# Two edits in a fused attention and gated-MLP training step: an early O^T load, and one finished input-gradient row per product

## The chip, the cores and the metric

The kernel runs on one core of one Trainium2 chip. A core has TensorE (PE, matrix products into PSUM), VectorE (DVE), ScalarE (ACT), GpSimd (POOL) and SyncE (SP). Here SP only starts DMA transfers, among them those that transpose while they copy; POOL starts the plain ones and does a few tiny copies. The metric is the device time of one execution in microseconds (us).

## The reference, cut to what matters

```python
xn = layernorm(x)                          # x: 2048 x 576
q = (xn @ wq) in 32 heads of 128           # k_cache, v_cache: 32 x 2048 x 128
p = softmax(q k^T / sqrt(128));  o = p v   # per head
s = concat(o) @ wo                         # 2048 x 4096 times 4096 x 576
g = silu((sigmoid(xn @ w_gate) * (xn @ w_up)) @ w_down)
out_0 = x + s * g
out_1..out_8 = vjp for x, k_cache, v_cache, wq, wo, w_gate, w_up, w_down of grad_out
```

So the kernel does the forward pass and the whole backward pass. out_1 is the gradient of the input x, and it goes back through the layernorm. out_4 is the gradient of wq, out_5 that of wo.

## The kernel before, in words

The 2048 rows are 16 row tiles of 128 (NT = 16). The stages, in order of time:

1. Up to about 3535 us: layernorm, the gated MLP's forward pass, and then attention, forward and backward, head by head. For each head it writes O and dQ in natural layout to DRAM (`on2_d`, `dq2_d`).
2. The O*wo stage, about 3535 to 3687 us. For each row tile, s = O wo is a sum over 32 heads (L957), each a pair of matmuls 512 and 64 columns wide. The stationary operand is O^T, so each row tile's O (128 x 4096, 1 MB) is loaded with a transposing DMA (`load_oT`, issued on SP, shown at L584).
3. The MLP's backward pass, in 18 column blocks, about 3687 to 4552 us.
4. The gradients of wq and wo and the rest of the input gradient, in 8 groups of 4 heads (NHG = 8, HG = 4), to the end.

**The O*wo stage.** Three O^T tiles rotate in memory whose contents are dead by now: row tile 0's lies in KQ, row tile 1's in xnT, row tile 2's in xn_all (the profile shows these names). KQ's first load is issued during attention. The wo rows of 23 heads (`h_early`) were loaded during attention, into dsT and xnT; those of the other nine (`h_late`) go to Kn, Vn and dOn, which attention still reads, so they are loaded in this stage (L575, on POOL). PE's order is written by hand: the early heads of row tile 0, the early heads of row tile 1, then the late heads of row tile 0, `close(0)`, the early heads of row tile 2, the late heads of row tile 1, and so on; from row tile 3 on a tile's heads go in one run. `close(st)` evicts the sums, starts the load of O^T for row tile st+3 into the same buffer, and forms out_0.

Before the first loads POOL issues `row_loads(0)` (three small row loads: dsg, g2b, xb). Then, for row tiles 1 and 2, it does a one-element copy from a loaded row into the O^T tile (L941), and only then is that O^T tile loaded: the copy makes SP's transposing load wait until the small load has landed. POOL issues the late wo rows after both copies.

**The last stage.** For each group of heads, SP loads the transposed wq columns (`wqT`, which lies in wdT's memory) and turns the dQ columns into `dqbT` four row tiles at a time (`turn_rows`; four calls for 16 row tiles). In every group PE does eight products of 32 matmuls (`accumulate`, L997): for each head one for wq's gradient (the result dqT is copied out by ACT, transposed into dwq by SP, and stored once a group by POOL) and one for wo's gradient (dwo, copied out by ACT and stored by POOL). Then it adds the group's part of the input gradient: 16 rows of `dx_more`, 8 matmuls each (L1053), which DVE adds to dxn.

In the last two groups rows are ended among the products. In group 6 (`early`) rows 0 to 7 get the parts of group 6 and of group 7 in one sum (16 matmuls), for which wqT2 and dqbT2, group 7's operands, are loaded ahead; rows 8 to 15 are added to dxn after the products. In group 7 (`final`) rows 8 to 15 get the last part and are ended. `finish` ends a row: on DVE tot and junk (two sums over the row), m12 and nb, then t; on ACT t again (scale and bias); on DVE dx; then POOL stores dx and loads a later row of grad_out. `ends_rows` decides when. It is called after each product but the last, and from product `wait_n` on it spreads the rows left over the places left, rounded up:

```python
if todo_rows and step_n >= wait_n:
    for _ in range(-(-len(todo_rows) // max(1, nsteps - step_n - final))):
```

With nsteps = 8, before: in group 6 (wait_n 5) after products 5, 6, 7: 3, 3, 2 rows; in group 7 (wait_n 2) after products 2 to 6: 2, 2, 2, 1, 1 rows.

The sums of products and rows rotate through four PSUM buffers. In these stages the program order fixes the instruction order on SP, POOL, DVE and PE; ACT's order is chosen by the scheduler when the program is built.

Of the kernel before, what the change touches and what calls it, by code (L numbers as in the profile page):

```python
# [66 lines left out]
def kernel(  # L67
# [6 lines left out]
    nc = tc.nc  # L74
# [6 lines left out]
    NT = S // P  # L81
# [152 lines left out]
    with tc.tile_pool(name="pa", bufs=1) as pa:  # L234
# [271 lines left out]
        with tc.tile_pool(name="a2h", bufs=3) as hp, \  # L506
# [4 lines left out]
            for sg in range(NT // SG):  # L511
# [7 lines left out]
                for sl in range(SG):  # L519
                    st = sg * SG + sl  # L520
# [358 lines left out]
    HG = ldiv(H, 4)  # L879
    NHG = H // HG  # L880
    WD = ncs[-1][0] + 512
    with late("pc") as pc, late("pcf") as pcf, \
# [22 lines left out]
        with late("c1l3", 4) as ldp3, late("c1s", 2) as sb, \  # L905
                late("c1ps", 3, space=PSUM) as ps, late("c1pt", 2, space=PSUM) as pst:
            if KPAD:
                nc.vector.memset(doBT[:LO, DT - 1, :], 0.0)

            def turn_do(st, pt):  # L910
                cols = slice(st * P, (st + 1) * P)
                for i in range(DT):
                    c0 = min(i * P, D - P)
                    nc.tensor.transpose(pt[:, i, :], doB[:, st, c0:c0 + P], ident[:])
                nf = DT - 1 if KPAD else DT
                if nf:
                    alt.copy(doBT[:, :nf, cols], pt[:, :nf, :], eng="s")
                if KPAD:
                    alt.copy(doBT[LO:, nf, cols], pt[LO:, nf, :], eng="v")

            wo_of = {}
            for view, h0, n, _ in wo_parts:
                for k in range(n):
                    wo_of[h0 + k] = view[:, k, :]
            h_early = [h0 + k for _, h0, n, dead in wo_parts if dead not in (1, 2, 3) for k in range(n)]
            h_late = [h0 + k for _, h0, n, dead in wo_parts if dead in (1, 2, 3) for k in range(n)]
            oTs.append(oT_view(xn_all[:].rearrange("p t d -> p (t d)"), 0))

            def row_loads(st):
                res = []  # L930
                for nm, src in (("dsg", dsg_d), ("g2b", g2_d), ("xb", x2)):
                    t_ = ldp3.tile([P, D], bf, name=nm)
                    nc.gpsimd.dma_start(t_[:], src[st * P:(st + 1) * P, :])
                    res.append(t_)
                return res

            R0 = min(3, NT)
            loads = {}
            loads[0] = row_loads(0)
            for st in range(1, R0):  # L940
                nc.gpsimd.tensor_copy(oTs[st][0:1, 0, 0:1], loads[0][st % 3][0:1, 0:1])  # L941
                load_oT(oTs[st], st)
            for view, h0, n, dead in wo_parts:
                if dead in (1, 2, 3):
                    load_wo_rows(view, h0, 0, n)
            for st in range(1, R0):
                loads[st] = row_loads(st)
            pend_tr = []
            accs_of = {}

            def mm(st, hs_):
                if st not in accs_of:
                    accs_of[st] = [ps.tile([P, 512], f32, name=f"acc{j}") for j in range(len(ncs))]
                oT = oTs[st % 3]
                for h in hs_:
                    for j, (n0, nn) in enumerate(ncs):
                        nc.tensor.matmul(accs_of[st][j][:, :nn], lhsT=oT[:, h, :], rhs=wo_of[h][:, n0:n0 + nn],  # L957
                                         start=(h == h_early[0]), stop=(h == (h_early + h_late)[-1]))

            def close(st):  # L960
                accs = accs_of.pop(st)
                dsg, g2b, xb = loads.pop(st)
                if st + R0 < NT:
                    load_oT(oTs[st % 3], st + R0)
                    loads[st + R0] = row_loads(st + R0)
                s_sb = sb.tile([P, D], f32, name="s_sb")
                for j, (n0, nn) in enumerate(ncs):
                    alt.copy(s_sb[:, n0:n0 + nn], accs[j][:, :nn], eng="s")
                nc.vector.tensor_tensor(doB[:, st, :], s_sb[:], dsg[:], op=ALU.mult)
                t0 = sb.tile([P, D], f32, name="t0")  # L970
                nc.vector.tensor_tensor(t0[:], s_sb[:], g2b[:], op=ALU.mult)
                nc.vector.tensor_tensor(xb[:], t0[:], xb[:], op=ALU.add)
                nc.gpsimd.dma_start(o0[st * P:(st + 1) * P, :], xb[:])
                pend_tr.append(st)

            for st in range(R0 - 1):
                mm(st, h_early)
            for st in range(NT):
                if st == NT - 3 or (st == 0 and NT < 3):
                    load_wdT(0)  # L980
                if st == NT - NT // 4:
                    load_blk(ah0[:, 0, :, :], a_d, 0)
                    load_blk(ah0[:, 1, :, :], h_d, 0)
                while len(pend_tr) > 1:
                    st_ = pend_tr.pop(0)
                    turn_do(st_, pst.tile([P, 8, P], bf, name="pt", tag="tr"))
                mm(st, h_late if st in accs_of else h_early + h_late)
                close(st)
                if st == 0 and R0 > 1:
                    mm(R0 - 1, h_early)  # L990
# [56 lines left out]
        def turn_rows(dst, src, a, b, n):  # L1047
            nc.sync.dma_start_transpose(dst[:, a * n:b * n, :], src[:, a:b, :].rearrange("p t f -> p (t f)"))
# [111 lines left out]
        with late("c2w") as wp, late("c2b") as blk, late("c2s", 2) as sb, late("c2ps", 4, space=PSUM) as ps:  # L1160
# [45 lines left out]
            for hg in range(NHG):  # L1206
                cols = slice(hg * HC, (hg + 1) * HC)
                onb, dqb = onqs[hg % 2]
                final = hg == NHG - 1
                early = hg == NHG - 2  # L1210
                ends = list(range(NTE)) if early else list(range(NTE, NT)) if final else []
                nc.sync.dma_start_transpose(wqT, A_wq[:, cols])
                for a in range(NTE if final else 0, NT, NQ):
                    turn_rows(dqbT, dqb, a, min(a + NQ, NT), HG)
                dwq = wp.tile([P, DT, HC], bf, name="dwq")
                for st in ends[:2]:
                    load_got(st)
                nsteps, step_n = 2 * HG, 0
                wait_n = min(5 if early else 2, nsteps - 2)
                todo_rows = list(ends)  # L1220
                held = []

                def ends_rows():
                    if todo_rows and step_n >= wait_n:
                        for _ in range(-(-len(todo_rows) // max(1, nsteps - step_n - final))):
                            if todo_rows:
                                st = todo_rows.pop(0)
                                finish(st, dx_more(st, early))
                                if st + 2 <= ends[-1]:
                                    load_got(st + 2)  # L1230
                for hl in range(HG):
                    h = hg * HG + hl
                    lcols = slice(hl * P, (hl + 1) * P)
                    accumulate(ps.tile([P, WD], f32, name="acc"), dqb, xn_all, lcols, dqTs[h % 2])
                    nc.sync.dma_start_transpose(dwq[:, :, lcols], dqTs[h % 2][:])
                    if early and hl == min(1, HG - 1):
                        nc.sync.dma_start_transpose(wqT2[:], A_wq[:, (hg + 1) * HC:(hg + 2) * HC])
                        turn_rows(dqbT2, onqs[(hg + 1) % 2][1], 0, NTE, HG)
                    if final and hl == HG - 1:
                        store_T(out_4, cols, dwq)  # L1240
                    step_n += 1
                    ends_rows()
                    dwo = sb.tile([P, D], bf, name="dwo")
                    accumulate(ps.tile([P, WD], f32, name="acc"), onb, ds_all, lcols, dwo)
                    nc.gpsimd.dma_start(out_5[h * P:(h + 1) * P, :], dwo[:])  # L1245
                    step_n += 1
                    if hl < HG - 1:
                        ends_rows()
                if not final:
                    if hg + 2 < NHG:  # L1250
                        load_on(onb, hg + 2)
                        load_dq(dqb, hg + 2)
                    store_T(out_4, cols, dwq)
                    for st in range(len(ends), NT):
                        acc = dx_more(st)
                        nc.vector.tensor_tensor(dxn[:, st, :], acc[:, :D], dxn[:, st, :], op=ALU.add)  # L1256
                while todo_rows:
                    step_n = nsteps
                    ends_rows()
# [30 lines left out]
```

## Time and profile before

| what | us |
|---|---|
| median of 4 runs | 4957.46 |
| the runs | 4955.02 to 4962.40 |
| the profiled execution's own time | 4957.68 |
| its span (first to last instruction) | 4955.9 |
| PE busy | 4839.2 |
| DVE busy | 2802.6 |
| ACT busy | 2472.1 |
| group 6 begins on PE | 4834.73 |
| group 7 begins on PE | 4903.69 |

How to read it: times in the trace count from the span's start. A line of a timeline has start, length, engine, line of the kernel, operation, output tile, input tiles, and, in brackets, how long the engine had been idle and what released it. A line of the waits has the engine and what it was about to do, the releaser, the total wait in us, the number of waits, and the longest. A line of the DMA issues has the tile, the queue, the count, the size where it is known, and the median us from issue to landing. The granted clock is the share of TensorE's full clock in a window. The rows' times come from one execution, so sums are made against its own time.

### The profile page before, as it was taken

The numbers are of one execution on the slowest core, as the hardware profiler recorded it, in microseconds if no ns is written. First come the engines' busy times: TensorE is split into PE (matmuls) and PEld (weight loads), VectorE is DVE, ScalarE is ACT, GpSimd is POOL, SyncE is SP. The second block draws the span as 40 slices with busy tenths as digits, with TensorE's granted clock in tenths as the row PEclk, the third lists the DMA queues.
The fourth block names the chain that finished last, engine by engine and source line by source line (L and its number), as shares of the span: only waits on it lengthen the run. The fifth ranks groups of instructions, "written<-read, shape, count | busy, mean of one in ns | idle before, by whom it ended". The sixth has DMA issues, their size and how long they took to land. (4 is left out here: it accounts for less than half of the span.)

```text
span 4955.9 us, 100870 instructions
## 1 busy us (share of the span) xinstructions
PE 4839.2 (98%) x40273; PEld 2895.1 (58%) x41029; DVE 2802.6 (57%) x6554; ACT 2472.1 (50%) x4228; POOL 840.8 (17%) x1330
## 2 busy tenths in 40 slices
PE   9999999999999999999999999999799999999998
PEld 4445666666666666666666666666455555555554
DVE  4544665666566566666666656656334555553224
ACT  4432766666766676676666666667212111111111
POOL 3322111111111111111111111111121111111111
PEclk9999999999999999999999999999899999999999
DMA  7887999999999999999999999999999999997765
GB/s 259 274 202 175 224 230 223 223 226 234 220 234 230 222 232 228 225 227 222 233 226 227 227 225 231 232 218 230 203 220 243 220 229 215 240 235 185 205 177 129
DMA packets 3048180, 1097.68 MB, mean 221 GB/s; under 512 B 2951889, under 2 KB 2956114, under 8 KB 3047698
## 3 DMA queue, kind: packets, MB, share of 16 engines
q1 hardware_dynamic: 2948930, 771.66, 83.3%
q0 software_dynamic: 98160, 318.85, 20.1%
q8 instruction: 322, 5.28, 0.4%
q14 instruction: 160, 1.31, 0.1%
q10 hardware_dynamic: 608, 0.59, 0.0%
HBM read 175.31 MB, written 177.93 MB: 71 GB/s over the span
## 5 line engine op out<-in xcount | busy, mean ns | idle before, releaser
L654 ACT ACTIVATE Pq<-sp 128x1024 bf16<-128x1024 f32 x1024 | 1047.0, 1023 | 269.4 <-PE sp L636 226.5
L709 DVE SCALAR_TENSOR_TENSOR Pq<-dp,negdelta,Pq 128x1024 bf16<-128x1024 f32 x512 | 655.2, 1280 | 42.4 <-PE dp L706 41.4
L712 ACT ACTIVATE t<-dp,negdelta 128x1024 bf16<-128x1024 f32 x512 | 567.1, 1114 | 214.5 <-PE dp L706 165.1
L683 PEld LDWEIGHTS <-dST 128*128 128x128 bf16 x8192 | 508.3, 98 | 150.9 <-DMA dST<-Pq 9.1
L706 PE MATMUL dp<-VT,dOT 128*128 128x512 bf16 x1919 | 581.6, 379 | 2.4
L683 PEld LDWEIGHTS <-PT 128*128 128x128 bf16 x8192 | 500.1, 98 | 135.5 <-DMA PT<-Pq 15.6
L636 PE MATMUL sp<-KQ 128*128 128x512 bf16 x1858 | 568.3, 379 | 2.2 <-ACT Pq L654 2.1
L683 PE MATMUL acc<-Kn,dST 128*128 128x128 bf16 x8192 | 557.1, 219 | 7.8 <-DMA dST<-Pq 5.9
L683 PE MATMUL acc<-Vn,PT 128*128 128x128 bf16 x8192 | 542.3, 219 | 12.6 <-DMA PT<-Pq 10.4
L744 PE MATMUL acc<-Pq,dOn 128*128 128x512 bf16 x1983 | 528.3, 379 | 10.2 <-issue 0.2
L713 DVE TENSOR_TENSOR Pq<-t,Pq 128x1024 bf16<-128x1024 bf16 x512 | 354.4, 692 | 318.9 <-ACT t L712 307.1
L744 PE MATMUL acc<-Pq,Qn 128*128 128x512 bf16 x2013 | 524.3, 380 | 4.9
L724 ACT ACTIVATE dq_n<-acc,rsc 128x128 bf16<-128x128 f32 x512 | 187.5, 366 | 332.5 <-PE acc L683 311.1
L1153 DVE TENSOR_TENSOR dxn<-acc,dxn 128x576 f32<-128x576 f32 x272 | 206.1, 758 | 248.1 <-PE acc L1053 248.1
L744 PEld LDWEIGHTS <-Qn 128*128 128x128 bf16 x2048 | 200.5, 98 | 240.9 <-issue 1.6
L744 PEld LDWEIGHTS <-dOn 128*128 128x128 bf16 x2048 | 199.2, 98 | 234.4 <-issue 1.1
L1115 ACT ACTIVATE ndh<-dh 128x512 bf16<-128x512 f32 x144 | 86.0, 597 | 452.5 <-DVE du_blk L1113 448.7
L706 PEld LDWEIGHTS <-dOT 128*128 128x128 bf16 x2048 | 178.9, 98 | 124.8 <-issue 12.7
L636 PEld LDWEIGHTS <-KQ 128*128 128x128 bf16 x2048 | 179.2, 98 | 124.1 <-issue 3.6
L641 DVE TENSOR_REDUCE rs_all<-rsp 128x1 f32<-128x2 f32 x512 | 78.4, 153 | 306.1 <-ACT Pq L654 294.6
L677 POOL DMA_DIRECT2D on_d<-o_n x128 | 97.1, 759 | 786.0 <-DVE junk L695 458.7
L677 POOL DMA_DIRECT2D dq_d<-dq_n x128 | 97.9, 765 | 718.1 <-ACT dq_n L724 678.3
(209 smaller groups left out, 6797.1 us busy)
## 6 DMA issues: line engine op xcount, KB each, us to landing
out_dram<-kvn POOLq DMA_DIRECT2D x64, 512.0 KB, 5.0
ah<-a_d POOLq DMA_DIRECT2D x18, 1024.0 KB, 9.2
ah<-h_d POOLq DMA_DIRECT2D x18, 1024.0 KB, 11.5
h_d<-h_row POOLq DMA_DIRECT2D x64, 256.0 KB, 3.5
a_d<-a_row POOLq DMA_DIRECT2D x64, 256.0 KB, 3.9
x_all<-in_A_k_cache_dram SPq DMA_DIRECT2D x64, 256.0 KB, 4.0
on_d<-o_n POOLq DMA_DIRECT2D x128, 128.0 KB, 4.6
kvT_d<-KQ POOLq DMA_DIRECT2D x32, 512.0 KB, 5.0
```

The costliest lines, as they stand in the source:

```text
L636: nc.tensor.matmul(sp[:, c * CH:(c + 1) * CH], lhsT=hs.QT[:, qt * P:(qt + 1) * P], rhs=hs.KT[:, hf * HW_ + c * CH: hf * HW_ + (c + 1) * CH ...
L654: nc.scalar.activation(Pq[:, hsl], sp[:], AF.Exp, scale=SCALE, accum_out=hs.rsp[:, hf:hf + 1])
L677: nc.gpsimd.dma_start(dst_d[q0 * P:(qt + 1) * P, hs.h * P:(hs.h + 1) * P].rearrange("(t p) d -> p t d", p=P), buf[:])
L683: nc.tensor.matmul(hs.acc[:, 0, :], lhsT=T[:, kt, :], rhs=rhs[:, kt, :], start=(kt == 0), stop=(kt == NT - 1))
L706: nc.tensor.matmul(dp[:, c * CH:(c + 1) * CH], lhsT=hs.dOT[:, qt * P:(qt + 1) * P], rhs=hs.VT[:, hf * HW_ + c * CH: hf * HW_ + (c + 1) * C ...
L709: nc.vector.scalar_tensor_tensor(Pq[:, hsl], dp[:], hs.negdelta[:, qt:qt + 1], Pq[:, hsl], op0=ALU.add, op1=ALU.mult)
L712: nc.scalar.activation(t[:], dp[:], AF.Identity, bias=hs.negdelta[:, qt:qt + 1], scale=1.0)
L713: nc.vector.tensor_tensor(Pq[:, hsl], t[:], Pq[:, hsl], op=ALU.mult)
L724: nc.scalar.activation(hs.dq_n[:, qt % G4, :], hs.acc[:, 0, :], AF.Copy, scale=hs.rsc[:, qt:qt + 1])
L744: nc.tensor.matmul(self.acc, lhsT=self.nat[:, qt, :], rhs=self.slabs[qt][:, cs], start=(qt == self.lo), stop=(qt == self.hi - 1))
L1115: nc.scalar.mul(ndh[:], dh[:], -1.0)
L1153: nc.vector.tensor_tensor(dxn[:, st, :], acc[:, :D], dxn[:, st, :], op=ALU.add)
```

## The change

In the O*wo stage, POOL's one-element copy is left out for row tile 1, so its O^T load no longer waits for a row load; row tile 2's is kept. In the last stage `wait_n` goes from 5 to 3 in group 6 and from 2 to 1 in group 7, so rows are ended after products 3 to 7 in group 6 (2, 2, 2, 1, 1 rows) and after products 1 to 6 in group 7 (2, 2, 1, 1, 1, 1). In group 6, SP's order is changed for that: the turns of dQ for rows 0 to 7, wqT2 and dqbT2 are issued at the group's start, and the turns for rows 8 to 15 after the second dwq transpose.

```diff
--- before.py
+++ after.py
@@ -938,7 +938,8 @@
             loads = {}
             loads[0] = row_loads(0)
             for st in range(1, R0):
-                nc.gpsimd.tensor_copy(oTs[st][0:1, 0, 0:1], loads[0][st % 3][0:1, 0:1])
+                if st > 1:
+                    nc.gpsimd.tensor_copy(oTs[st][0:1, 0, 0:1], loads[0][st % 3][0:1, 0:1])
                 load_oT(oTs[st], st)
             for view, h0, n, dead in wo_parts:
                 if dead in (1, 2, 3):
@@ -1210,13 +1211,18 @@
                 early = hg == NHG - 2
                 ends = list(range(NTE)) if early else list(range(NTE, NT)) if final else []
                 nc.sync.dma_start_transpose(wqT, A_wq[:, cols])
-                for a in range(NTE if final else 0, NT, NQ):
-                    turn_rows(dqbT, dqb, a, min(a + NQ, NT), HG)
+                def turn_dq(a, b):
+                    for a_ in range(a, b, NQ):
+                        turn_rows(dqbT, dqb, a_, min(a_ + NQ, b), HG)
+                turn_dq(NTE if final else 0, NTE if early else NT)
+                if early:
+                    nc.sync.dma_start_transpose(wqT2[:], A_wq[:, (hg + 1) * HC:(hg + 2) * HC])
+                    turn_rows(dqbT2, onqs[(hg + 1) % 2][1], 0, NTE, HG)
                 dwq = wp.tile([P, DT, HC], bf, name="dwq")
                 for st in ends[:2]:
                     load_got(st)
                 nsteps, step_n = 2 * HG, 0
-                wait_n = min(5 if early else 2, nsteps - 2)
+                wait_n = min(3 if early else 1, nsteps - 2)
                 todo_rows = list(ends)
                 held = []
 
@@ -1234,8 +1240,7 @@
                     accumulate(ps.tile([P, WD], f32, name="acc"), dqb, xn_all, lcols, dqTs[h % 2])
                     nc.sync.dma_start_transpose(dwq[:, :, lcols], dqTs[h % 2][:])
                     if early and hl == min(1, HG - 1):
-                        nc.sync.dma_start_transpose(wqT2[:], A_wq[:, (hg + 1) * HC:(hg + 2) * HC])
-                        turn_rows(dqbT2, onqs[(hg + 1) % 2][1], 0, NTE, HG)
+                        turn_dq(NTE, NT)
                     if final and hl == HG - 1:
                         store_T(out_4, cols, dwq)
                     step_n += 1
```

## The prediction

> **What bounds the kernel now.** I read the page first (what is busy), then PE's waits inside the two stages the diff touches, then the timelines of PE, SP and DVE there. The page:
>
> ```profile
> span 4955.9 us, 100870 instructions
> PE 4839.2 (98%) x40273; PEld 2895.1 (58%) x41029; DVE 2802.6 (57%) x6554; ACT 2472.1 (50%) x4228; POOL 840.8 (17%) x1330
> ```
>
> TensorE fills the span, so only what removes its idle time, or the tail after its last matmul, can pay. The waits of PE in the O*wo stage (3530 to 3690 us) and in the last two head groups (4834 to 4956):
>
> ```profile
> PE acc L957 <- DMA xnT<-on_d: 18.9, 1, 18.9
> ...
> PE acc L1053 <- DMA dqbT<-dqb: 3.8, 1, 3.8
> PE acc L1053 <- DVE dxn L1256: 3.2, 1, 3.2
> PE acc L1053 <- DVE tot L1192: 1.1, 1, 1.1
> ```
>
> The first line is the second O^T tile (its view lies in xnT's memory); the rest belong to group 6, the last but one. SP's own waits, and what was in flight from 3536 to 3562 (last number: us to landing):
>
> ```profile
> SPq L584 <- POOL xn_all L941: 10.9, 1, 10.9
> ...
> Kn<-in_A_wo_dram POOLq DMA_DIRECT2D x1, 432.0 KB, 9.6
> Vn<-in_A_wo_dram POOLq DMA_DIRECT2D x1, 432.0 KB, 12.8
> dOn<-in_A_wo_dram POOLq DMA_DIRECT2D x1, 432.0 KB, 13.3
> xnT<-on_d SPq DMA_TRANSPOSE x1, 17.9
> xn_all<-on_d SPq DMA_TRANSPOSE x1, 22.2
> ```
>
> SP issued xnT's load at 3542.40 and had been held 10.9 us by the Pool copy: it stood ready at 3531.5. PE's timeline of group 6 (start, length, last bracket the idle time before):
>
> ```profile
> 4854.33 1.14 PE L1053 MATMUL acc<-wdT,dqbT 128*128 128x512 bf16 x8
> 4859.24 2.10 PE L1053 MATMUL acc<-wqT,dqbT 128*128 128x512 bf16 x8 [3.77 <-DMA dqbT<-dqb]
> ...
> 4892.76 1.14 PE L1053 MATMUL acc<-wdT,dqbT 128*128 128x512 bf16 x7 [1.11 <-DVE tot L1192]
> 4897.10 6.75 PE L1053 MATMUL acc<-wdT,dqbT 128*128 128x512 bf16 x32 [3.20 <-DVE dxn L1256]
> 4903.69 4.08 PE L997 MATMUL acc<-xn_all,dqb 128*128 128x512 bf16 x31
> ```
>
> A product starts every 3.92 us, a half row (8 matmuls) every 0.98. After the 3.77 and the 3.20 wait matmuls run at half speed.
>
> **Part 1, O*wo.** Removed: one Pool copy (0.18 us, off the path) and SP's wait. The built order shows no other difference in this stage. SP is ready at 3531.5; the load's issue takes 4.89. Landing: 7.0 us at the least and 10.0 at the median for these loads, so 3538.5 to 3541.5. In flight beside it are only the kvT_d store (issued 3535.36) and the first row loads (3539.19). PE needs the tile when row 0's early part ends, 3541.5, so the 18.94 us wait goes (1 us left at most).
>
> What is late next: row 1's early 23 heads take 5.65 us, to 3547.2. Row 0's late heads then need the wo loads, which Pool still issues behind the copy for xn_all: Kn 3543.24+9.6=3552.8, Vn 3556.8, dOn 3558.0, then 0.74 us, 3558.8. Row 2's early part needs xn_all. Its load now goes out at 3543.0, where xnT's went before, into the same burst of wo and row loads. Upper bound: xnT's 17.9, landing 3560.9 (3562 if the row loads land 1 us later beside xnT). Lower: the median 10.0, but not before the late heads, 3555.5. Nearest row is the burst itself, with no second transpose queued behind it: I take 3559.7. Row 2's early part started at 3570.30 before: 10.6 earlier.
>
> A clock cost comes off. After its 18.94 us wait row 1's early part took 7.62 us (3560.47 to 3568.09) instead of 5.65: 2.0 lost, already in the old time. Now PE idles from 3547.2 to 3552.8 and works in pieces, so row 2's early part pays: 2.3 (2.0 to 3.4, half of the 6.8 us slow stretches seen). It ends at 3559.7+5.65+2.3=3567.65 against 3570.30+5.65=3575.95: **8.3 us gained**, between 4.9 (3562, 3.4) and 12.8 (3555.5, 2.0). Later rows lie beside their loads: row 3's load goes out when row 0 closes, near 3558.9, and landed 9.4 us after issue before, 3568.3, needed near 3572.5. Everything after shifts with PE, which had 1.9 us of waits in all from 3570 to group 6.
>
> The page "DMA: Bandwidth & Descriptors" of the Trainium skill (Queues, rings and completion order) says each DMA engine takes turns between queues packet by packet; here transposes move in packets under 512 B and wo loads in larger ones, so by that rule xn_all gains nothing from xnT's absence, lands at 3560.9, and this part's gain would be 7.1. The trace can't separate the two.
>
> **Part 2, group 6.** Matmuls and DVE's list are unchanged; two row pairs move ahead on PE, ACT's copies and Pool's dwo stores are reordered around the rows, and on SP wqT2 and dqbT2 pass two dqb turns and two dwq transposes. Pure PE work is 8x3.92+16x0.98+8x0.98=54.9; the group took 4903.69-4834.73=68.96: 14.1 lost (waits 3.77+1.11+3.20; half clock 7.74x0.38=2.9 after the first and 6.60x0.42=2.8 after the last, by the granted clocks below). New order on SP from 4834.93: wqT 3.77, two turns 2.03+1.96, wqT2 2.90, dqbT2 4.24, with gaps 4850.1; PE resumed 1.8 after dqbT2's issue ended, so 4851.9. PE has three products done at 4846.49 and a half row at 4847.47, so **it still waits, 4.4 instead of 3.8**, and pays the half clock once (2.9 as before, up to 3.4; I take 3.1). Rows then come two per product for three products, one for two, 34.9 us of DVE chain (8 rows of 4.36, below) beside 4851.9 to 4889: PE's four PSUM buffers, each freed by a row's tot or by ACT's copy, are free in time (the 1.11 and 3.20 waits were for them, behind three rows at once), so these waits and the second slow stretch go. If the chain lagged by one row again, 1.1 would be back. 54.9+4.4+3.1=62.4: **6.6 gained**. The dwq transposes that waited now end 4852.7, long before dqT's buffers are wanted (4869); the two delayed turns land at 4859, wanted at 4889. Pool's dwo stores stand behind two rows' stores instead of three, and dwo's two buffers are wanted two products later.
>
> ```profile
> 4925.12 0.76 DVE L1202 TENSOR_TENSOR dx<-t,got 128x576 bf16<-128x576 f32 x1 [0.99 <-ACT t L1200]
> 4925.80 0.75 DVE L1192 SCALAR_TENSOR_TENSOR tot<-acc,dxn 128x576 f32<-128x576 f32 x1
> ...
> 4929.47 0.76 DVE L1202 TENSOR_TENSOR dx<-t,got 128x576 bf16<-128x576 f32 x1 [0.99 <-ACT t L1200]
> ```
>
> One row holds DVE for 4.36 us, ACT's step included.
>
> **Group 7.** From its start: wqT 2.31, first turn 2.08, landing and restart 2.2 and gaps: the first rows' data are there at +6.85. PE is there at +3.92, one product earlier than before, so a **new wait of 2.9** appears; behind it PE holds seven products. The row chain starts at +8.05 instead of +9.02 (4912.71): 1.0 gained. The end gives it back: ACT's built order now puts the last dqT copy behind row 15's t. From that t's end: copy 0.62, dwq transpose 2.7 to landing, 0.3, two out_4 issues 1.3, then the dwo store, 4.9; before, 4946.87 to 4949.88, 3.0. So +1.9-1.0=**0.9 lost**, 1.5 if the new wait also slows PE, since the first row then takes up to 1 us longer.
>
> Weighing that: the windows show granted clock 0.62 after the 3.77 wait, 0.58 after the 3.20 wait, and 1.00 from 504.28 after a 2.33 wait; 2.9 lies between, even odds. "TensorE: Matmul & The Clock Gate" of the Trainium skill (Part 1) puts the drop at one idle window of about 3.4 us that runs freely, a rule that speaks against cutting a wait into new ones; by it 2.9 us would cost nothing and group 7 loses 0.9, by the nearest row (3.20) 1.5.
>
> Late stage: 6.6-1.2=5.4 gained, between 2.8 (dqbT2 2 us later, a slow stretch of 3.4, 1.5 in group 7) and 6.5 (dqbT2 0.8 sooner, 0.9 in group 7).
>
> **Sum.** The profiled execution took 4957.68 (span 4955.9), 0.2 over the median 4957.46. 4957.68-8.3-5.4=4944.0: **4944**.
>
> **Rivals.** (A) Forecast: 4938.4 to 4950 at the ends of both parts. (B) xn_all and the wo loads land later still, near 3565, and O*wo gives 3: 4949.3. For: both are still held, and 22.2 us to landing occurs. Against: in the trace that figure has xnT's load in front of it. (C) Group 6's wait grows by 5 (dqbT's longest landing is 10.0 us against a median of 4.3): 4949. For: dqbT2 now runs where two turns did. Against: the only large load near it, dqb's, landed at 4822.25+14.2=4836.5. (D) Slower: xnT in flight starves the first row loads, whose landing releases the Pool copy and so wo and xn_all. Its price is one for one; O*wo breaks even at a delay of 8.3 us, the whole change at 13.7. If xnT takes xn_all's 22.2 (to 3553.7) and the rows land after it, the copy is 13.7 late, O*wo loses 5.4, and with the late part at its 2.8 the time is 4960.3. Against: the DMA share is 0.40 from 3535 to 3541.5, not the burst's 1.01. (E) The load isn't early, since another wait holds SP: 4952.3. Against: its remaining waits are on stores and transposes of attention that landed by 3531.
>
> **Numbers.** A 0.78, B 0.08, C 0.08, D 0.03, E 0.03. A measurement of this kernel tells about 0.2% (9.9 us) from no change, so faster means under 4947.6. A lies there for 92 in 100, B and C for a third: 0.78x0.92+0.16/3=0.77. Slower by that much is the far end of D, 0.02; the rest, 0.21, is the same. The range, 4938 to 4951, runs from A's lower end over B and C; D, E and their neighbours are left out.
>
> **What would show it.** Right: xnT issued near 3531.5; PE's 18.9 wait replaced by one near 3547 for the wo loads, 5 to 12 us in all with xn_all; in group 6 one wait of 4 to 5 us on dqbT2, none on tot or dxn; in group 7 a wait near 3; out_4 issued last behind a late dqT copy. Wrong: xnT or the copy late, a PE wait on dqT or dwo copies, or more than two slow stretches in the late stage.

## The result, and the profile after

The changed kernel takes 4946.15 us (median of 44 runs, 4940.76 to 4958.83); the kernel before, run beside it, 4957.46 us (median of 65, 4946.28 to 4971.02). The ratio is 0.9978, 95% interval 0.9974 to 0.9982: faster by 0.22%, 11 us. The forecast was 4944 us, 13.7 less than the profiled execution of before. The profiled execution of the changed kernel took 4943.66 us.

The page, then PE's waits in the O*wo stage (3530 to 3690 us) and in the last two groups (4815 to 4942), after the change:

```profile
span 4941.8 us, 100865 instructions
PE 4836.5 (98%) x40273; PEld 2893.3 (59%) x41029; DVE 2802.9 (57%) x6554; ACT 2471.8 (50%) x4228; POOL 840.6 (17%) x1329
...
PE acc L958 <- issue: 4.7, 3, 3.2
PE acc L958 <- DMA Vn<-in_A_wo_dram: 3.4, 1, 3.4
PE acc L958 <- DMA Kn<-in_A_wo_dram: 2.4, 1, 2.4
PE acc L958 <- DMA xn_all<-on_d: 1.2, 1, 1.2
...
PE acc L1054 <- DMA dqbT<-dqb: 6.3, 2, 3.8
```

The 18.9 us wait for xnT is gone, and the waits for the wo loads and xn_all that the forecast put in its place are there: 5.8 and 1.2, 7.0 in all. Not forecast is "issue": three stops, the longest 3.2, in which PE waited for nothing that the profile shows. In the last two groups one wait of 3.8 (group 6) and one of 2.5 (group 7) are left, both for dqb turns.

Attention ends at another time in every execution (3526 to 3545 us here), so the stage is measured from there. The O*wo stretch, from attention's last matmul to the MLP backward's first, went from 153.30 to 147.93 us; group 6 from 68.96 to 61.45; group 7's start to the span's end from 52.19 to 53.23. So 5.4 + 7.5 - 1.0 = 11.9 us; attention, whose instructions the change does not touch, ended 2.2 us sooner in this pair. That the profiled time, 4943.66, falls on the forecast's 4944.0 is luck: without those 2.2 us it would lie 2 us above it.

### The profile page after: what moved, and what is told of

The parts are those of the page before. It is cut to its first block, busy times and chain, and to the rows that moved or that the text cites. A ratio compares the mean times of both kernels' runs of the same rounds, so it can differ in the third digit from the quotient of the medians.

```text
span 4941.8 us, 100865 instructions
## 1 busy us (share of the span) xinstructions
PE 4836.5 (98%) x40273; PEld 2893.3 (59%) x41029; DVE 2802.9 (57%) x6554; ACT 2471.8 (50%) x4228; POOL 840.6 (17%) x1329
## 4 chain that ended last, share of the span: by engine, by line
PE 93%; issue 2%; DMA 2%; DVE 2%; ACT 0%; SPq 0%; POOL 0%; POOLq 0%; ACTq 0%; DVEq 0%
PE acc L683 18%; PE acc L744 17%; PE acc L998 12%; PE acc L1054 8%; PE dp L706 8%; PE sp L636 8%; PE acc L215 6%; PE u_ps L450 3%; PE dh L1111 3%; PE g_ps L448 3%; PE acc L533 2%; PE acc L958 2%; PE acct L145 1%; DMA PT<-Pq 1%; DVE Pq L709 1%
## 5 line engine op out<-in xcount | busy, mean ns | idle before, releaser
L744 PE MATMUL acc<-Pq,dOn 128*128 128x512 bf16 x1983 | 527.8, 379 | 10.0
L744 PE MATMUL acc<-Pq,Qn 128*128 128x512 bf16 x2013 | 522.9, 379 | 4.9
L744 PEld LDWEIGHTS <-Qn 128*128 128x128 bf16 x2048 | 200.1, 98 | 240.0
L744 PEld LDWEIGHTS <-dOn 128*128 128x128 bf16 x2048 | 198.9, 98 | 234.2 <-issue 0.5
```

Source lines behind the costliest of these rows:

```text
L744: nc.tensor.matmul(self.acc, lhsT=self.nat[:, qt, :], rhs=self.slabs[qt][:, cs], start=(qt == self.lo), stop=(qt == self.hi - 1))
```

## The new stop behind attention

PE and POOL after the change (start, length; last bracket the idle time before), with the same places of the kernel before in the second fence; the L744 line ends attention:

```profile
3529.74 2.32 PE L744 MATMUL acc<-Pq,Qn 128*128 128x512 bf16 x10
...
3533.40 2.61 PE L958 MATMUL acc<-dsT,KQ 128*128 128x512 bf16 x20 [1.35 <-issue]
3539.23 2.56 PE L958 MATMUL acc<-dsT,KQ 128*128 128x512 bf16 x10 [3.21 <-issue]
...
3556.65 1.60 PE L958 MATMUL acc<-Vn,KQ 128*128 128x512 bf16 x6 [3.37 <-DMA Vn<-in_A_wo_dram]
...
3560.86 6.73 PE L958 MATMUL acc<-dsT,xn_all 128*128 128x512 bf16 x33 [1.18 <-DMA xn_all<-on_d]
...
3540.06 0.55 POOL L933 DMA_DIRECT2D dsg<-dsg_d  x1 [6.36 <-issue]
...
3544.20 0.18 POOL L942 COPY xn_all<-xb 1x1 bf16<-1x1 bf16 x1 [2.52 <-DMA xb<-in_A_x_dram]
```

```profile
3531.94 2.32 PE L744 MATMUL acc<-Pq,Qn 128*128 128x512 bf16 x10
...
3538.19 1.88 PE L957 MATMUL acc<-dsT,KQ 128*128 128x512 bf16 x13 [0.56 <-issue]
...
3539.19 0.55 POOL L933 DMA_DIRECT2D dsg<-dsg_d  x1 [3.28 <-issue]
...
3542.74 0.18 POOL L941 COPY xn_all<-xb 1x1 bf16<-1x1 bf16 x1 [0.37 <-DMA xb<-in_A_x_dram]
```

POOL stood 6.36 us instead of 3.28 ahead of its first row load. PE stopped 3.21 instead of 0.56 in the middle of row 0's early heads, for which everything was loaded. Counted from attention's end, POOL's first row load comes 3.1 us later than before, and the copy that releases xn_all and the wo loads comes 12.1 us after it (3544.20 - 3532.06) instead of 8.5 (3542.74 - 3534.26): 3.7 later. What was in flight (last number: us to landing):

```profile
q14 instruction: 9, 0.07, 0.8%
q8 instruction: 3, 0.05, 0.6%
...
Kn<-in_A_wo_dram POOLq DMA_DIRECT2D x1, 432.0 KB, 7.2
Vn<-in_A_wo_dram POOLq DMA_DIRECT2D x1, 432.0 KB, 11.2
dOn<-in_A_wo_dram POOLq DMA_DIRECT2D x1, 432.0 KB, 11.7
xnT<-on_d SPq DMA_TRANSPOSE x1, 10.6
xn_all<-on_d SPq DMA_TRANSPOSE x1, 16.3
```

At the end of attention the engines leave a branch, and two queues of kind "instruction" move packets between 3528 and 3562 us. xnT's load, issued at 3529.92, now runs just then. Theory F: it slows the engines' instruction loads behind the branch. Rival G: the stops belong to the place in the program, or to chance.

## The experiments

Besides the ratio, each kernel's profiled execution is read by these stretches (us):

| kernel | O*wo stretch | attention's end to row 2 | row 2's early part | group 6 | group 7 to the end |
|---|---|---|---|---|---|
| before | 153.30 | 36.04 | 5.63 | 68.96 | 52.19 |
| changed | 147.93 | 28.80 | 8.04 | 61.45 | 53.23 |
| owo_only | 145.33 | 28.61 | 5.63 | 68.01 | 52.15 |
| ends_only | 152.75 | 33.31 | 8.35 | 62.00 | 53.36 |
| xnT_after_branch | 148.54 | 30.38 | 7.06 | 60.88 | 53.34 |
| no_hold | 136.51 | 19.78 | 5.64 | 62.11 | 53.26 |
| wo_first | 149.67 | 31.16 | 7.41 | 58.76 | 53.78 |
| both_after_branch | 156.06 | 37.33 | 7.64 | 58.92 | 53.69 |
| wqT2_up | 148.04 | 29.79 | 7.16 | 57.45 | 53.47 |
| g7_two | 146.87 | 30.14 | 5.63 | 61.05 | 52.30 |
| best1 | 136.18 | 19.46 | 5.63 | 56.88 | 52.26 |
| best2 | 142.95 | 26.22 | 5.64 | 56.89 | 52.15 |

**The two parts apart.** `owo_only` is the kernel before with the `if st > 1:` alone, `ends_only` the changed kernel without it.

> The kernel before with the O*wo edit alone (the second O^T tile's load not held); the last two head groups as before. In the pair of traces the stretch from attention's last matmul to the first matmul of the MLP backward went from 153.30 to 147.93 us. Theory T (the traces' split: the edit is worth 5.4 us, because new stops right after attention, 3.2 us on PE and 3.1 us more on POOL, took back part of what was forecast): ratio 0.9989, that stretch 148 us, PE's stop of about 3 us with no visible releaser inside row 0's early part, POOL idle about 6.4 us ahead of its first row load. Rival P (the forecast's 8.3 us; the one profiled execution showed less by chance): ratio 0.9983, the stretch 145 us, the stops as in the profile before (0.6 on PE, 3.3 on POOL). Rival Z (the two parts are worth something only together): ratio above 0.9995.

> The changed kernel with the held load put back, so the last two head groups' edits alone. Theory T (the traces' split): group 6 lasts 61.5 us instead of 69.0, group 7 to the span's end 53.2 instead of 52.2, together 6.5 gained, ratio 0.9987; O*wo stretch 153.3 us with PE's wait of about 19 us for the second tile. Rival P (the forecast's sizes): 6.6 - 1.2 = 5.4 gained, ratio 0.9989, with a wait of 4.4 on dqbT in group 6 and, at even odds, a slow stretch of the clock behind group 7's new wait. The two differ by 1.1 us, so the groups' lengths in the trace tell more than the ratio.

owo_only: 4955.76 us, ratio 0.9993 (0.9984 to 1.0002); ends_only: 4952.50, ratio 0.9988 (0.9978 to 0.9997). Their product, 0.9981, fits the whole change's 0.9978: the parts add. The intervals are too wide to size either part (owo_only's even holds 1), but the stretches do: O*wo took 145.3 to 148.0 us in the four executions with the edit as it was made (changed, owo_only, wqT2_up, g7_two; mean 147.0) and 153.0 in the two without, a gain of 6.0. Both stops are there again in owo_only (2.87 and 6.12). In ends_only PE waited 10.91 us for xnT, not the 19 expected, and then 4.91 for xn_all, in nearly the same stretch: how the lost time splits between the two tiles changes from execution to execution.

**Is it the load beside the branch?** One more instruction on POOL puts xnT's load behind the branch:

```
+            nc.gpsimd.memset(oTs[1][0:1, 0, 0:1], 0.0)
             loads[0] = row_loads(0)
```

> The changed kernel with one Pool memset of one element of the second O^T tile put ahead of Pool's first row load, so the tile's load goes out when Pool has come past the branch, instead of some 10 us sooner, and not behind the row loads as before. Theory F (the stops after attention come from the load's transfer running while the engines fetch their instructions behind the branch): POOL's idle time before its first work is back near 3.3 us from 6.4, PE's stop in row 0's early part back near 0.6 us from 3.2, the copy for the third tile and the three late wo loads 3 us sooner after attention's end; the second tile's load goes out about 6 us after attention's end and lands 8 to 11 us later, so PE waits 2 to 6 us for it instead; the stretch from attention to the MLP backward lasts 145 to 149 us against 147.9, ratio to the kernel before 0.9972 to 0.9979. Rival G (the stops belong to the branch or to chance, not to the transfer): POOL's idle time stays near 6.4 us or varies freely, the tile's load goes out 9 us after attention's end, and PE waits 6 us or more for it on top of the 3.2: stretch 150 to 154 us, ratio 0.9982 to 0.9990.

POOL's and PE's timelines:

```profile
3530.77 0.09 POOL L939 MEMSET xnT<- 1x1 bf16 x1 [2.09 <-issue]
...
3540.50 0.18 POOL L943 COPY xn_all<-xb 1x1 bf16<-1x1 bf16 x1 [7.63 <-DMA xb<-in_A_x_dram]
...
3531.64 1.87 PE L959 MATMUL acc<-dsT,KQ 128*128 128x512 bf16 x14 [0.73 <-POOL xnT L939]
...
3540.82 7.20 PE L959 MATMUL acc<-dsT,xnT 128*128 128x512 bf16 x34 [5.84 <-POOL xn_all L943]
```

The stops went, 2.09 on POOL and 0.73 on PE, as theory F says. But the stage gained nothing: PE stopped 5.84 us later on, at the first matmul that reads xnT (the profile names the copy that ended about then), and the row loads, now beside xnT's load, kept the copy waiting 7.63, so that it came 1.3 us later after attention's end than in the changed kernel (13.5 against 12.1) and not 3 sooner. The stretch, 148.54, lies in F's forecast; the ratio, 0.9987 (0.9978 to 0.9996), lies in G's, and its interval reaches down to F's, so it does not decide. Over all the kernels the split is clean: where xnT's load runs through the branch (changed, owo_only, no_hold, wo_first, wqT2_up, g7_two, best1) PE's stop is 2.66 to 5.13 and POOL's 6.12 to 7.88; where it doesn't (before, ends_only and three kernels that move it) PE's is at most 0.92 and POOL's 2.09 to 3.28.

The instruction packets say the same. In the first 4 us after attention's end the kernel before moves these (3534.26 to 3538.26: queue, packets, MB, share of the DMA engines), and the changed kernel (3532.06 to 3536.06) none:

```profile
q14 instruction: 3, 0.02, 2.1%
q8 instruction: 1, 0.02, 1.7%
```

The five kernels without xnT's load in flight move 4 to 6 such packets in those 4 us, the first 1.2 us after attention's end; the seven with it move none, and their first comes 4.4 to 5.1 us after it. So the packets are late by about as much as the engines. That the engines stand for these packets still isn't measured itself; the times fit it in all twelve kernels.

**The hold that was left.** `no_hold` takes away the other copy too, so xn_all's load follows xnT's at once; `wo_first` keeps it and issues the wo loads ahead of the row loads.

```
             for st in range(1, R0):
-                if st > 1:
-                    nc.gpsimd.tensor_copy(oTs[st][0:1, 0, 0:1], loads[0][st % 3][0:1, 0:1])
                 load_oT(oTs[st], st)
```

> The changed kernel with the third O^T tile's load (into xn_all) not held either, so SP issues it right behind the second's, about 3 us after attention's end, and Pool issues the late wo loads without first waiting 2.5 us for the row loads' landing. Theory H (a held load only costs; its traffic finds room): PE's 1.2 us wait for xn_all goes, the waits for Kn and Vn (2.4 + 3.4) shrink by about 2.7, and the stretch from attention to the MLP backward is 144 us against 147.9, ratio to the kernel before 0.9970. Theory F with D (a transfer beside the instruction fetch lengthens the stops, and the row and wo loads are starved by two transposes): POOL idle 8 us or more ahead of its first row load, PE's stop 3 us or more, Kn landing no sooner than before: stretch 148 to 154 us, ratio 0.9978 to 0.9990.

> The changed kernel with the three late wo loads issued by Pool ahead of the first row loads; the third tile's load still held behind the row loads. It asks why taking that hold away saved 11.4 us (stretch from attention to the MLP backward 147.9 with the hold, 136.5 without). Theory X (the third tile's own lateness set row 2, and its transfer beside the wo loads slowed those): Kn, Vn and dOn land 6 to 8 us after issue, PE's waits for them fall from 5.8 to 1 us or less, but the row loads land behind 1.3 MB, the copy comes 3 to 6 us later, and PE stops 5 to 9 us for the third tile: stretch 145 to 151 us. Rival N (what counted was that the wo loads no longer stood behind the copy): stretch 141 us or less.

no_hold: 4937.63 us, ratio 0.9952 (0.9938 to 0.9965), twice the change's gain. PE's timeline and the wo landings of no_hold, then of wo_first:

```profile
3544.83 1.88 PE L956 MATMUL acc<-dsT,KQ 128*128 128x512 bf16 x14 [3.36 <-issue]
...
3554.07 0.90 PE L956 MATMUL acc<-Kn,KQ 128*128 128x512 bf16 x6 [0.26 <-DMA Kn<-in_A_wo_dram]
...
3557.33 4.33 PE L956 MATMUL acc<-dsT,xn_all 128*128 128x512 bf16 x34
...
Kn<-in_A_wo_dram POOLq DMA_DIRECT2D x1, 432.0 KB, 6.6
Vn<-in_A_wo_dram POOLq DMA_DIRECT2D x1, 432.0 KB, 7.1
```

```profile
3560.43 6.11 PE L958 MATMUL acc<-dsT,xn_all 128*128 128x512 bf16 x34 [8.48 <-DMA xn_all<-on_d]
...
Kn<-in_A_wo_dram POOLq DMA_DIRECT2D x1, 432.0 KB, 4.6
Vn<-in_A_wo_dram POOLq DMA_DIRECT2D x1, 432.0 KB, 5.6
```

Without the hold the stretch is 136.5 us. That is 11.4 less than in the changed kernel and 7.5 less than even theory H asked for, although both stops are there (3.36, and 6.67 on POOL). xn_all is there when row 2 wants it; Vn lands in 7.1 us instead of 11.2, since the transposed load is issued by then (SP 3541.20 to 3547.54, Kn from 3547.48); and row 2 runs at full clock (5.64 instead of 8.04), though it also did so behind the longer waits of owo_only and g7_two (5.63). wo_first shows the other side: with nothing transposed beside them the wo loads land in 4.6 to 6.1 us, sooner than X's 6 to 8, and PE waits for none of them, yet the stretch is 149.7, because xn_all is 8.48 us late. So xn_all's hold bounded the stage, as theory X says; the wo loads' place did not. (wo_first's time, one run: 4940.45.)

**Can the stop be had away as well?** `both_after_branch` is no_hold with the memset above, so both transposed loads go out behind the branch. `best2` issues xnT's load inside attention and holds xn_all's by such a memset; it also has best1's edits of the last groups (below).

> The version without the holds, but with a one-element Pool memset of the second tile ahead of the first row load, so that the second and, behind it, the third O^T tile's loads go out when Pool has come past the branch. Theory F: PE's stop inside row 0's early part 1 us or less and POOL's idle time 2 to 3.3 us, but the second tile now goes out near 4 us after attention's end and lands 8 to 11 us later, so PE waits 4 to 7 us for it at the end of row 0's early part, and the row loads beside it land 3 to 8 us later than without: stretch from attention to the MLP backward 138 to 143 us, worse than the 136.5 of the version whose loads run through the branch. Rival G (the stops come anyway): the wait for the tile comes on top of them, 143 us or more.

> The version with no hold, wqT2 in group 5 and group 7 at two products, with two further edits: the second O^T tile's load is issued inside attention, and the third's is held by a one-element Pool memset ahead of the first row load, so that it goes out only when Pool has come past the branch. So no O^T load runs while the engines come past the branch. Theory F (a running transfer lengthens those stops; with it 2.7 to 5.1 us on PE inside row 0's early part and 6.1 to 7.9 on POOL, without it at most 0.9 and 3.3): PE stops 1 us or less there, POOL idles 2 to 3.3 us, row 2's early part starts 15 to 18 us after attention's end instead of 19.5, stretch from attention to the MLP backward 131 to 134 us against 136.2; attention's end may come 0 to 5 us later, as SP now issues 5 us of load among attention's transposes. Ratio 0.9935 to 0.9950. Rival G (the stops belong to the place in the program): PE's stop stays near 3, POOL's near 6, stretch 136 us or more, ratio above 0.9945. Rival S (SP has no room for the load inside attention): the stretch falls, but attention's end comes more than 5 us later, ratio above 0.9950.

The waits of both_after_branch in the stage, then PE and two landings of best2:

```profile
PE acc L957 <- DMA xnT<-on_d: 12.4, 1, 12.4
PE acc L957 <- DMA xn_all<-on_d: 7.4, 1, 7.4
...
PE acc L957 <- issue: 0.4, 1, 0.4
```

```profile
3567.57 1.60 PE L958 MATMUL acc<-Kn,KQ 128*128 128x512 bf16 x6 [9.11 <-DMA Kn<-in_A_wo_dram]
...
Kn<-in_A_wo_dram POOLq DMA_DIRECT2D x1, 432.0 KB, 15.4
xn_all<-on_d SPq DMA_TRANSPOSE x1, 19.1
```

The stops go in both (0.4 and 0.85 on PE), and both lose. both_after_branch: 156.1 us in the stage, 13 past the most that F allowed and without the stops that G asked for, one run 4947.73. best2: 4944.19 us, ratio 0.9969 (0.9961 to 0.9978) against best1's 0.9945, because the wo loads, issued 2 us after xn_all's instead of at its end, took 15.4 to 16.6 us. The O*wo stretch holds 6.8 of the 12 us between the two ratios. Its PE also waited 7.1 us for a transpose inside attention, and its attention ended at 3545, six after the latest of the others: rival S had a share, of which no run tells the size. So the load in flight lengthens the stops, as F says, but what F gave for taking it away was wrong. In no_hold the longer stop also keeps POOL's loads back until the transposed ones are out (Kn from 3547.48, xn_all's issue to 3547.54); without it they collide.

**The last two groups.**

```
+                if hg == max(0, NHG - 3) and NHG > 1:        # group 5
+                    nc.sync.dma_start_transpose(wqT2[:], A_wq[:, (NHG - 1) * HC:NHG * HC])
...
                 if early:
-                    nc.sync.dma_start_transpose(wqT2[:], ...)   # the same load in group 6
```

> The changed kernel with the load of the last group's weights (wqT2) issued by SP at the start of group 5 instead of inside group 6, so that in group 6 the dqbT2 turn follows the first two dqb turns at once. Theory Q (the 3.8 us wait left in group 6 is SP's queue: wqT, two turns, 2.6 us of wqT2, 4.3 us of dqbT2): the wait falls to 1.1 us, group 6 from 61.5 to 58.8 us, and to about 56 if the slow stretch of the clock behind the wait goes too; group 5 (47.0 us) is unchanged because its own turns are wanted only at its end. Rival (the wait is for data of dqb that come late, or the transposes themselves become slower next to each other): the wait stays between 3 and 4 us and group 6 at 61 to 62 us.

The second edit is `wait_n = min(3 if early else 2, nsteps - 2)`.

> The changed kernel with group 7 as before (first row after two products instead of one); group 6 as changed. By the prediction's own steps the row chain then starts 1.3 us later than the 7.74 us of the changed kernel, and ACT's last dqT copy is back ahead of row 15's step, so that from that step's end to the last store it takes 3.0 us again instead of 5.35: group 7's start to the span's end 52.2 us instead of 53.2, and no wait of 2.5 us for the first turn. Rival (the loss at the end came from the rows' chain, not from ACT's order): 53 us or more.

Group 6's wait in the changed kernel, then in wqT2_up, then in wo_first, whose group 6 is the changed kernel's:

```profile
4843.85 0.66 PE L1054 MATMUL acc<-wqT,dqbT 128*128 128x512 bf16 x2 [3.79 <-DMA dqbT<-dqb]
...
4847.69 1.89 PE L1054 MATMUL acc<-wqT,dqbT 128*128 128x512 bf16 x8
```

```profile
4848.74 1.15 PE L1054 MATMUL acc<-wqT,dqbT 128*128 128x512 bf16 x8 [2.40 <-DMA dqbT<-dqb]
```

```profile
4842.72 1.15 PE L1054 MATMUL acc<-wqT,dqbT 128*128 128x512 bf16 x8 [3.71 <-DMA dqbT<-dqb]
```

In wqT2_up the wait falls by 1.4, not by the 2.6 of the moved issue, since SP's other issues took longer (dqbT2's 4.66 instead of 4.33, wqT's 3.99 instead of 3.76) and the landing half a us more. The clock is not slowed behind it (8 matmuls in 1.15 instead of 1.89), and group 6 lasts 57.45. Only the shorter wait is surely the edit's: in the seven executions with group 6 as changed the wait is 3.71 to 4.94, and in two of them (wo_first, both_after_branch) it did not slow the clock either, and the group lasted 58.8 and 58.9. One run: 4946.17. In g7_two the end is back at 52.30, as expected. The ends of the changed kernel (ACT, POOL) and of g7_two:

```profile
4929.64 0.87 ACT L1201 ACTIVATE t<-t,nb,rstd_all 128x576 f32<-128x576 f32 x1 [3.49 <-DVE t L1200]
4930.41 0.62 ACT L40 CAST dqT<-acc 128x576 bf16<-128x576 f32 x1
...
4934.58 0.76 POOL L1006 DMA_DIRECT2D out_dram<-dwq  x1 [2.45 <-DMA dwq<-dqT]
...
4935.86 0.57 POOL L1250 DMA_DIRECT2D out_dram<-dwo  x1
```

```profile
4933.03 0.62 ACT L40 CAST dqT<-acc 128x576 bf16<-128x576 f32 x1
4936.61 0.87 ACT L1201 ACTIVATE t<-t,nb,rstd_all 128x576 f32<-128x576 f32 x1 [2.97 <-DVE t L1200]
...
4940.48 0.57 POOL L1250 DMA_DIRECT2D out_dram<-dwo  x1
```

Behind row 15's t (its end at 4930.51) the changed kernel needs 5.35 us to the last store, with the dqT copy after t and POOL waiting 2.45 for its transpose; in g7_two the copy comes before t and it takes 3.00 (4937.48 to 4940.48). One run: 4948.39.

**Put together.** best1 is no_hold with these two edits.

> Neither the second nor the third O^T tile's load held, wqT2's load moved to group 5, and group 7's rows from the second product on. If the parts add: O*wo stretch 136.5 us, group 6 56 to 59 us, group 7 to the span's end 52.2, that is 17 us in O*wo, 10 to 13 in group 6, nothing lost in group 7 against the kernel before: ratio 0.9937 to 0.9946. Rival (the gains do not add, since each one only moves the wait to the next transfer): no better than the 0.9952 of the version without the hold alone.

best1: 4931.74 us, ratio 0.9945 (0.9933 to 0.9958), its profiled span 4921.9. The parts add: O*wo 136.18, group 6 56.88, group 7 52.26. It beats the kernel before by about 27 us, and its interval lies clear of the change's.

## Why the prediction was right, and where it was off

- **O*wo: 8.3 forecast, 5.4 in the pair, 6.0 over the executions.** xnT's load did go out early (3529.92) and landed in 10.6 us, its wait went, and the wo loads and xn_all came next with 7.0 us of waits, inside the 5 to 12 forecast. The step that failed is the one that kept POOL's copy where it was before ("Its load now goes out at 3543.0"). Counted from attention's end it came 3.7 us later, and by the forecast's own rule that costs one for one: 8.3 - 3.7 = 4.6. Rival D had that price, and the forecast left 3 in 100 for it; its cause was half right, as POOL waited 2.5 us for the row loads' landing instead of 1.9, and what grew most was its stop ahead of their issue. Both measured figures still lie in the forecast's 4.9 to 12.8. From issue, xn_all took 16.3 us where the forecast took 16.7 from the burst; the 17.9 that the prediction drew from "DMA: Bandwidth & Descriptors" of the Trainium skill (Queues, rings and completion order) was further off. The slow stretch was priced at 2.3 and cost 8.04 - 5.65 = 2.4 in the pair; in owo_only and g7_two, with like waits ahead of it, row 2's early part took 5.63 and there was none.
- **Group 6: 6.6 forecast, 7.5 measured.** One wait, 3.79 instead of 4.4 (3.71 to 4.94 over the seven executions); one slow stretch; no wait on tot or dxn.
- **Group 7: 0.9 to 1.5 lost forecast, 1.0 measured.** The wait was 2.47 (2.9 forecast), the row chain began at +7.74 (+8.05), out_4 went out behind the late dqT copy, with one dwo store after it (5.35 against 4.9). The 0.6 that a slow stretch was to add at the end was its most: in five of the kernels the clock dropped there (below), and the end came 0.0 to 0.6 us later than in the changed kernel.
- **The sum.** 13.7 forecast; 11.9 from the three stretches. O*wo's miss of 2.9 is partly made up by group 6's 0.9.

## What to carry to other kernels

Before a load is moved forward, look at what runs in the stretch that it is moved into, stops without a visible releaser included, and take later instructions' times from the new start of the stretch rather than from the old clock. A hold that keeps one transfer behind another is worth testing away as a whole: here half of it was removed for 6 us, and the other half was worth 11 more. When transfers collide, their order decides: the same three wo loads took 5 to 6 us alone, 7 to 8 right behind a transposed load's issue, 7 to 12 issued with one, and 15 to 17 issued 2 us after one.

## What the runs showed of the hardware that was not expected

- Behind the branch at attention's end POOL stood 2.1 to 3.3 us and PE up to 0.9 us, and with a transposing load in flight 6.1 to 7.9 and 2.7 to 5.1. The first instruction packets came 1.2 us after attention's end without such a load and 4.4 to 5.1 with it. That the engines wait there for their instructions was not measured itself. "Runtime: NRT & Kernel Launch" of the Trainium skill (Instruction fetch mechanics) says that a taken branch out of the fetched window stops an engine until a DMA has fetched the target; the instruction packets in this stretch fit it.
- Which waits slow PE's clock isn't a matter of their length alone. In group 7 a wait of 2.47 us left the 16 matmuls behind it at 2.13 us in the changed kernel, and behind a wait of the same 2.47 in wo_first they took 3.60. In group 6 waits of 3.71 and 3.86 left it at full speed, and one of 3.79 did not. Granted clock (the number ahead of the DMA share) behind the wait in the changed kernel, then behind no_hold's wait of 2.52:

```profile
4895.20:4902.00 6.80, 6.75 (x55) 3.48 (x56) 4.51 (x11) 1.51 (x2) 0.91 (x2) 1.00 0.36 75
```

```profile
4889.90:4897.00 7.10, 7.10 (x45) 3.38 (x46) 4.77 (x12) 0.87 (x1) 1.07 (x2) 0.76 0.35 79
```

  By the rule of "TensorE: Matmul & The Clock Gate" of the Trainium skill (Part 1), one idle window of about 3.4 us, which the prediction weighed, no wait of 2.5 us should have slowed it (so the rule speaks for cutting a long wait into short ones, not against it as the prediction has it). The measurement decides, and the prediction's even odds between the rows were the better reading.
